# Bucket products as four 32-row pieces, key hashes side by side, and three PSUM banks for the preparing steps

## Chip, cores and metric

The kernel runs on one core of one Trainium2 chip. Its metric is the device time of one execution in microseconds (us). Executions of one kernel agree within about 0.2%, and every run told here with more than one execution is in the fast state. A ratio is the mean time of one kernel's fast runs over that of the other's fast runs of the same rounds, so it is not quite the ratio of the medians that are quoted beside it.

## The reference, cut to what matters

```python
# q, k, v: 4 batches x 8 heads x 768 x 64;  proj: 64 x 6
q_bucket = sum((q @ proj > 0) * 2**arange(6));  k_bucket likewise      # one of 64 buckets
scores   = where(q_bucket == k_bucket, q @ k.T / 8, -1e9)
attn     = softmax(scores) @ v
x        = attn of all heads, as (3072, 512)
out      = (silu(x @ w_gate) * (x @ w_val)) @ w_out                    # 512 -> 1536 -> 512
```

The bucket test is done by a matmul. A query has 13 numbers per head (six signs twice and a constant), and a key has 13 numbers of the order of 2^35. Their product is zero where all six bits agree and hugely negative otherwise. It is accumulated in PSUM ahead of the f32 scores, and the exponential then turns the excluded entries into zero.

## The kernel before

Work goes by pairs of heads, and within a pair by "rounds": two chunks of 128 keys against 384 queries, for both heads. While a pair is attended, the next pair is prepared: transposes of queries and keys, then their hashes. FFN products of the previous batch ("atoms") are woven in between, but during the first batch there are none.

```python
mm_ps  = tile_pool(bufs=2, space=PSUM)     # bank():      FFN products
aux_ps = tile_pool(bufs=1, space=PSUM)     # side_bank(): preparing steps and row sums
sc_ps  = tile_pool(bufs=2, space=PSUM)     # two chunks' scores, two banks each

def front(n, bank=side_bank):              # the steps that prepare pair n
    def transpose(name, half):
        ps = bank("tps")
        for i in range(CH): nc.tensor.transpose(ps[:, i*P:(i+1)*P], raws[name, n][...], ident)
        nc.scalar.copy(T[name, n][:, half*HQ:(half+1)*HQ], ps[:, 0:HQ])
    def hash_bits(name, half):
        ps = bank("hps")
        nc.tensor.matmul(ps[:, 0:HQ], hash_w[name], T[name, n][:, cols], start=True, stop=True)
        # q: sign on ScalarE; k: compare and scale on VectorE, into bf16 bits
    ...                                    # 4 transposes, then 4 hashes (q, k, q, k)

def score(u):                              # one chunk of keys; a round calls it twice
    sc = sc_ps.tile([P, 2, 512], FP32, tag="sc", name="sc")
    for x, start in ((bits, True), (T, False)):
        for h in range(2):
            rows = slice(h * D, (h + 1) * D)              # 64 rows a head, both products
            nc.tensor.matmul(sc[:, h, 0:HQ], x["k", n][rows, ks], x["q", n][rows, qs],
                             start=start, stop=not start)
    nc.scalar.activation(ring[u % RING][:, :, 0:HQ], sc[:, :, 0:HQ], AF.Exp, scale=SCALE)

def norm(u):                               # every third round
    ps = side_bank("sum")                  # row sums: matmuls with ones, 64 columns a head
    ...
    nc.vector.reciprocal(r, ps[:, 0:HQ])   # holds side_bank
# ... attend (weighted sums), FFN, weight narrowing on VectorE, main loop left out
```

The softmax here doesn't subtract the row's maximum and nothing guards it: scores larger than these inputs give would overflow.

## Time and profile before

| | before |
|---|---|
| time, median of 4 | 1187.30 us |
| first score | 13.25 us |
| first stretch (first score to first FFN product) | 130.1 us |
| first FFN product of first batch to that of the second | 287.4 us |
| FFN part (first FFN product to the end of the last product) | 1038.9 us |

How to read it: TensorE sets the time, so the kernel falls into a start (data arrives, first pair prepared), a first stretch (attention alone, TensorE sometimes waits) and an FFN part (TensorE never idle, up to the last down-projection). The limits are starts of groups in TensorE's timeline; the prediction shows the stretches themselves. The start, in TensorE's timeline of the kernel before (start in us, length, what, how often, idle before):

```profile
4.79 0.87 PE L205 MATMUL tps<-ident,qraw 128*128 128x128 f32 x3 [4.79 <-DMA qraw<-in_q_dram]
...
6.62 0.87 PE L205 MATMUL tps<-ident,kraw 128*128 128x128 f32 x3 [0.95 <-DMA kraw<-in_k_dram]
...
13.25 0.34 PE L244 MATMUL sc<-qb,kb 64*128 64x384 bf16 x2
```

Queries arrive at 4.8 us and keys at 6.6. Three transposes take 0.87 us here and 0.55 once the array runs at full clock.

### The profile page before, as it was taken

The numbers are of one execution on the slowest core, as the hardware profiler recorded it, in microseconds if no ns is written. First come the engines' busy times: TensorE is split into PE (matmuls) and PEld (weight loads), VectorE is DVE, ScalarE is ACT, GpSimd is POOL, SyncE is SP. The second block draws the span as 40 slices with busy tenths as digits, with TensorE's granted clock in tenths as the row PEclk, the third lists the DMA queues.
The fourth block names the chain that finished last, engine by engine and source line by source line (L and its number), as shares of the span: only waits on it lengthen the run. The fifth ranks groups of instructions, "written<-read, shape, count | busy, mean of one in ns | idle before, by whom it ended". The sixth has DMA issues, their size and how long they took to land.

```text
span 1185.9 us, 10899 instructions
## 1 busy us (share of the span) xinstructions
PE 1156.9 (98%) x4480; PEld 573.2 (48%) x4480; DVE 508.2 (43%) x756; ACT 280.3 (24%) x441; POOL 19.2 (2%) x44
## 2 busy tenths in 40 slices
PE   7888899999999999999999999999999999999998
PEld 3333355555544445555554445555554444555543
DVE  3777689998852323343331233333233222222100
ACT  4444422222212222222221213222131211000000
POOL 0000000000000000000000000000000000000000
PEclk9999999999999999999999999999999999999999
DMA  5322222324210120100002012010000000000000
GB/s 142 76 76 76 58 79 92 101 71 113 88 40 18 37 57 1 40 1 1 14 1 58 18 36 49 1 40 1 14 1 1 18 18 18 1 1 0 1 27 27
DMA packets 63698, 44.76 MB, mean 38 GB/s; under 512 B 51872, under 2 KB 55968, under 8 KB 63648
## 3 DMA queue, kind: packets, MB, share of 16 engines
q1 hardware_dynamic: 58752, 26.23, 8.6%
q0 software_dynamic: 4896, 17.83, 4.9%
q8 instruction: 35, 0.57, 0.2%
q14 instruction: 15, 0.12, 0.0%
HBM read 37.76 MB, written 6.29 MB: 37 GB/s over the span
## 4 chain that ended last, share of the span: by engine, by line
PE 97%; DVE 2%; ACT 1%; DMA 0%; SPq 0%; issue 0%; ACTq 0%
PE val L299 21%; PE g L299 21%; PE po L320 21%; PE sc L244 14%; PE av L255 11%; PE hps L213 4%; PE sum L276 2%; PE tps L205 2%; DVE r L279 2%; ACT qb L216 0%; ACT qT L208 0%; DMA kraw<-in_k_dram 0%; SPq L85 0%; ACT A L246 0%; ACT o L324 0%
## 5 line engine op out<-in xcount | busy, mean ns | idle before, releaser
L299 PE MATMUL val<-xT,wv 128*128 128x384 f32 x768 | 266.2, 489 | 0.0
L299 PE MATMUL g<-xT,wg 128*128 128x384 f32 x768 | 265.9, 489 | 0.0
L320 PE MATMUL po<-wo,ht 128*128 128x512 f32 x576 | 257.1, 597 | 0.0
L246 ACT ACTIVATE A<-sc 128x768 f32<-128x768 f32 x192 | 155.5, 812 | 208.2 <-PE sc L244 177.0
L299 PEld LDWEIGHTS val<-xT,wv 128*128 128x128 f32 x768 | 142.5, 190 | 105.4 <-DVE acc L263 6.0
L299 PEld LDWEIGHTS g<-xT,wg 128*128 128x128 f32 x768 | 142.5, 190 | 105.1 <-DVE acc L263 6.0
L320 PEld LDWEIGHTS po<-wo,ht 128*128 128x128 f32 x576 | 106.8, 190 | 134.1 <-issue 130.7
L244 PE MATMUL sc<-qT,kT 64*128 64x384 f32 x768 | 156.0, 485 | 0.0
L279 DVE RECIPROCAL r<-sum 128x384 f32<-128x384 f32 x32 | 81.8, 2556 | 151.9 <-PE sum L276 151.9
L255 PE MATMUL av<-A,vraw 128*64 128x386 f32 x768 | 144.8, 498 | 0.0
L306 DVE SCALAR_TENSOR_TENSOR t<-t,g 128x384 f32<-128x384 f32 x96 | 53.1, 554 | 206.3 <-ACT t L305 206.3
L263 DVE TENSOR_TENSOR acc<-acc,A 128x768 f32<-128x768 f32 x128 | 122.3, 955 | 35.2 <-ACT A L246 30.3
L305 ACT ACTIVATE t<-g 128x384 f32<-128x384 f32 x96 | 47.1, 490 | 351.6 <-PE g L299 347.0
L311 DVE SCALAR_TENSOR_TENSOR ht<-t,val 128x384 f32<-128x384 f32 x96 | 53.1, 553 | 125.0 <-PE val L299 125.0
L255 PEld LDWEIGHTS av<-A,vraw 128*64 128x64 f32 x768 | 49.6, 137 | 82.4 <-issue 81.3
L244 PEld LDWEIGHTS sc<-qT,kT 64*128 64x128 f32 x768 | 69.0, 190 | 21.5 <-issue 21.5
L244 PE MATMUL sc<-qb,kb 64*128 64x384 bf16 x384 | 63.8, 329 | 0.1
L218 DVE TENSOR_SCALAR kb<-hps,above_k,times_k 128x384 bf16<-128x384 f32 x32 | 21.6, 675 | 83.9 <-PE hps L213 83.4
L244 PEld LDWEIGHTS <-kb 64*128 64x128 bf16 x384 | 18.7, 93 | 67.9 <-issue 55.1
L324 ACT COPY o<-po 128x512 f32<-128x512 f32 x24 | 14.0, 585 | 144.3 <-PE po L320 142.0
L216 ACT ACTIVATE qb<-hps,nudge 128x384 bf16<-128x384 f32 x32 | 18.6, 581 | 69.4 <-PE hps L213 69.3
L213 PE MATMUL hps<-qT,hashq 128*128 128x384 f32 x64 | 27.7, 515 | 5.5 <-DVE e L281 5.5
(58 smaller groups left out, 409.9 us busy)
## 6 DMA issues: line engine op xcount, KB each, us to landing
qraw<-in_q_dram SPq DMA_DIRECT2D x32, 192.0 KB, 3.7
kraw<-in_k_dram SPq DMA_DIRECT2D x32, 192.0 KB, 4.6
vraw<-in_v_dram SPq DMA_DIRECT2D x16, 384.0 KB, 3.4
words<-in_moe_w_val_dram POOLq DMA_DIRECT2D x12, 512.0 KB, 3.8
words<-in_moe_w_out_dram POOLq DMA_DIRECT2D x12, 512.0 KB, 3.6
out_dram<-o SPq DMA_DIRECT2D x24, 256.0 KB, 2.0
words<-in_moe_w_gate_dram POOLq DMA_DIRECT2D x10, 512.0 KB, 3.9
words<-in_moe_w_gate_dram SPq DMA_DIRECT2D x2, 512.0 KB, 5.8
```

Of the source, the lines that this page charges most:

```text
L205: nc.tensor.transpose(ps[:, i * P : (i + 1) * P], raws[name, n][:, half * CH + i, :, :].rearrange("p h d -> p (h d)"), ident)
L213: nc.tensor.matmul(ps[:, 0:HQ], hash_w[name], T[name, n][:, cols], start=True, stop=True)
L244: nc.tensor.matmul(sc[:, h, 0:HQ], x["k", n][rows, ks], x["q", n][rows, qs], start=start, stop=not start)
L246: nc.scalar.activation(ring[u % RING][:, :, 0:HQ], sc[:, :, 0:HQ], AF.Exp, scale=SCALE)
L255: nc.tensor.matmul(ps[h * D : (h + 1) * D, 0:AW], raws["v", n][:, h, c, :], a[:, h, :], start=c == 0, stop=c == NCH - 1)
L263: nc.vector.tensor_tensor(acc[n, half], acc[n, half], a[:, :, 0:HQ], op=ALU.add)
L279: nc.vector.reciprocal(r, ps[:, 0:HQ])
L299: nc.tensor.matmul(ps[:, 0:HQ], w[:, j, f * P : (f + 1) * P], x[:, j, half * HQ : (half + 1) * HQ], start=j == 0, stop=j == NJ - 1)
L305: nc.scalar.activation(t, ps[:, 0:HQ], AF.Tanh, scale=0.5)
L306: nc.vector.scalar_tensor_tensor(out=t, in0=t, scalar=1.0, in1=ps[:, 0:HQ], op0=ALU.add, op1=ALU.mult)
L311: nc.vector.scalar_tensor_tensor(out=ht, in0=now["t"], scalar=0.5, in1=ps[:, 0:HQ], op0=ALU.mult, op1=ALU.mult)
L320: nc.tensor.matmul(ps, hs[half][f][:, i * P : (i + 1) * P], wo[:, f, :], start=f == 0, stop=f == NF - 1)
```

## The change

Its intent: run four bucket products at once instead of two, hash both halves of the keys in one go, bring in the first data on two queues with the array warmed by idle products, and, while there is no FFN work, let the preparing steps take turns over three PSUM banks.

```diff
-    load(0)
+    load(0, nc.scalar)                  # first keys on ScalarE's queue
+    zeros = konst.tile([P, 512], BF16, ...); nc.vector.memset(zeros, 0.0)
+    for _ in range(9):
+        nc.tensor.matmul(bank("idle"), zeros[:, 0:P], zeros, start=True, stop=True)
     # hash weights: proj is loaded twice, then copied by VectorE to its ten places
     # (before: six small DMAs); 13 rows now every 32 partitions (before: every 64)
@@ front
+    def front_bank(name):
+        return side_bank(name) if atoms or next(turn) % 3 == 2 else bank(name)
-            ps = bank("tps")            # bank was side_bank, but for the first pair
+            ps = front_bank("tps")
+        def hash_k():
+            ps = front_bank("hps")
+            chunks = T["k", n].rearrange("p (i g t) -> p i g t", g=2, t=P)
+            for g in range(2):          # even chunks to rows 0-63, odd ones to rows 64-127
+                nc.tensor.matmul(ps[g*D:(g+1)*D, 0:HQ].rearrange(...), hash_w["k"],
+                                 chunks[:, :, g, :], start=True, stop=True)
+            nc.vector.tensor_scalar(bits["k", n], ps[:, 0:HQ], ...)     # one compare, not two
-        # steps: 4 transposes, hash q, hash k, hash q, hash k
+        return steps + [hash_k, lambda: hash_q(0), lambda: hash_q(1)]
@@ score, now once a round
+        sc = [sc_ps.tile([P, 2, 512], FP32, tag="sc", name="sc") for _ in range(2)]
+        for g in range(2):
+            for h in range(2):
+                rows = slice(g*D + h*QUART, g*D + (h+1)*QUART)          # 32 rows
+                nc.tensor.matmul(sc[g][:, h, 0:HQ], bits["k", n][rows, ...],
+                                 bits["q", n][rows, qs], start=True, stop=False)
+        for g in range(2):
+            ...                         # scores of chunk g, 64 rows a head, then its exponential
```

## The prediction

> **What bounds the kernel now.** I read the page (busy times, the chain that ended last), then busy times by stretch, then who kept TensorE waiting early on, then TensorE's instructions in order of time.
>
> ```profile
> PE 1156.9 (98%) x4480; PEld 573.2 (48%) x4480; DVE 508.2 (43%) x756; ACT 280.3 (24%) x441; POOL 19.2 (2%) x44
> PE 97%; DVE 2%; ACT 1%; DMA 0%; SPq 0%; issue 0%; ACTq 0%
> L244 PE MATMUL sc<-qb,kb 64*128 64x384 bf16 x384 | 63.8, 329 | 0.1
> ```
>
> TensorE is 97% of the chain, so only time in TensorE's stream counts, and the others where they hold it up. The third row is the bucket product: 63.8 us in all. Busy times by stretch (TensorE, weight loads, VectorE, ScalarE, GpSimd, clock, DMA):
>
> ```profile
> 13.25:143.37 130.12, 110.53 (x626) 46.06 (x625) 94.00 (x125) 58.31 (x84) 3.84 (x7) 0.99 0.29 78
> 143.37:340.00 196.63, 196.63 (x795) 103.61 (x794) 175.84 (x296) 48.70 (x79) 14.55 (x27) 1.00 0.30 87
> 340.00:996.00 656.00, 656.00 (x2516) 319.09 (x2514) 206.30 (x261) 153.34 (x241) 0.00 (x0) 1.00 0.08 21
> ```
>
> The first stretch is the first batch's attention, before there is any FFN work to fill in: TensorE has nothing in flight for 19.6 of 130 us. After it TensorE is never idle. VectorE is at 89% up to 340 us, so it has room there, but not much. TensorE's waits up to 113.6 us (total, times, longest):
>
> ```profile
> PE tps L205 <- DVE e L281: 4.1, 3, 1.4
> PE hps L213 <- DVE e L281: 4.1, 3, 1.4
> PE hps L213 <- ACT qb L216: 4.0, 6, 0.7
> PE tps L205 <- ACT qT L208: 4.0, 7, 0.6
> ```
>
> All are the preparing steps (transposes, hashes) of the next pair of heads, queueing for one PSUM bank, behind each other's copy or behind the reciprocal that reads the row sums. Now TensorE in order of time (start, length, what):
>
> ```profile
> 72.32 0.34 PE L244 MATMUL sc<-qb,kb 64*128 64x384 bf16 x2
> ...
> 75.49 0.34 PE L244 MATMUL sc<-qb,kb 64*128 64x384 bf16 x2
> ...
> 85.50 0.55 PE L205 MATMUL tps<-ident,qraw 128*128 128x128 f32 x3
> 86.61 0.55 PE L205 MATMUL tps<-ident,kraw 128*128 128x128 f32 x3 [0.57 <-ACT qT L208]
> 87.09 0.34 PE L244 MATMUL sc<-qb,kb 64*128 64x384 bf16 x2
> ```
> ```profile
> 301.61 2.85 PE L299 MATMUL g<-xT,wg 128*128 128x384 f32 x8
> 304.29 0.49 PE L205 MATMUL tps<-ident,qraw 128*128 128x128 f32 x3
> 304.62 2.75 PE L299 MATMUL val<-xT,wv 128*128 128x384 f32 x8
> 307.20 0.49 PE L205 MATMUL tps<-ident,kraw 128*128 128x128 f32 x3
> 307.53 2.75 PE L299 MATMUL g<-xT,wg 128*128 128x384 f32 x8
> 310.21 0.34 PE L244 MATMUL sc<-qb,kb 64*128 64x384 bf16 x2
> 310.38 0.81 PE L244 MATMUL sc<-qT,kT 64*128 64x384 f32 x4
> 311.03 0.33 PE L244 MATMUL sc<-qb,kb 64*128 64x384 bf16 x2
> 311.19 0.81 PE L244 MATMUL sc<-qT,kT 64*128 64x384 f32 x4
> 311.93 1.52 PE L255 MATMUL av<-A,vraw 128*64 128x386 f32 x8
> ```
>
> Read starts, not lengths, since ends overlap. A bucket pair (two heads) takes 0.16 to 0.17 us until the scores start, so the two heads already run side by side (384 columns at 2.4 per ns are 0.16). Eight FFN products before a transpose take 2.58; before the bucket products, with 128 rows going to 64, they take 2.68. Leaving a tile shape costs 0.10 us. The eight at 301.61, which follow 64-column products, also take 2.68, though a transpose of their own shape comes next: 0.10 us again, now on entry, where an f32 weight load (190 ns each) can't be hidden. Entering with bf16 weights (93 ns) costs 0.01.
>
> **What the Trainium skill says.** "TensorEngine Tiling (Array Packing)", Tiling Modes, Key Properties: "Changing tiling mode (not just tile) drains the TensorE". The 0.10 us above agrees, for 128 rows to 64 and for 64 columns to 128. No run yet shows 32 rows to 64. "TensorE: Matmul & The Clock Gate", Part 3, Measured speedup vs the span model: tiles in different row groups run together, some 4 ns apart, four 32-row tiles at 512 columns 3.07 times as fast. The trace has two at a time at full rate. Same page, Part 1, What's actually happening: TensorE starts at half clock and needs about 3.4 us of activity. The trace's first transposes agree (three take 0.87 us at 4.79, 0.55 later). The Tiling page, Gotcha 1: row tiles must write different PSUM banks; the four pieces do.
>
> **The change part by part.** A round is two chunks of two heads. There are 96, 25 of them start before 139.56 us and 71 later, nearly all beside FFN work.
>
> *Bucket products.* Four 64-row matmuls in two goes become four 32-row ones in one go: −0.163 us. But now 32-row tiles come before the 64-row scores, which had shared the old shape. By the rows above that adds 0.10 for leaving and 0.10 for the f32 weight load: +0.20. Net +0.04 us per round, so 71 × 0.04 = +2.8 us beside the FFN. If 32 to 64 rows doesn't drain, −0.163 per round instead.
>
> *Key hashes.* Two f32 hashes of 0.65 us each (two passes of 0.322) become one go of 0.65 with two 64-column tiles. Beside the FFN they now stand between 128-column products: two shape changes at 0.10, entries at 0.05 and 0.10, so 0.35 of the 0.65 is given back. −0.30 × 11 pairs = −3.3 us. VectorE does one compare of 0.675 us less per pair, off the path.
>
> *First stretch.* From round to round now: plain 3.17 (72.32 to 75.49), new 3.21. Two transposes add 1.59 (87.09 − 85.50); without waits three at 0.109 plus entry, drain and the second three are 0.33 + 0.48 = 0.81. A row sum adds 0.70. Key hash and first query hash add 0.645 + 0.645 + 0.10 + 0.10 = 1.49; the last query hash 0.85. One pair of heads is six rounds: 6 × 3.21 + 2 × 0.70 + 2 × 0.81 + 1.49 + 0.85 = 24.6 us, against 31.2 now (72.32 to 103.53). The first pair, lacking a row sum and one product, takes 22.5 against 27.9. One step in three still uses the row sums' bank. Counting the turns, four steps follow a row sum there: two first ones wait 1.35 us and two second ones 1.0, together 4.7. So to 139.56: 22.5 + 3 × 24.6 + 4.7 + 3.2 = 104.2 against 126.3. VectorE then bounds almost as tightly: per pair eight adds of 0.955 and two of 0.95, two reciprocals of 2.556, 1.4 of normalising, 0.675, and thirteen weight-narrowing steps of 0.576: 24.2 us against 24.6. I add 1 us of stumbling: **−21 us**.
>
> *Start.* The first score is at 13.25. Queries and keys come at 4.8 and 6.6 us while the DMA share is about 1; two queues share the bandwidth, so I take both at 6.5. Nine idle products (half clock, 0.43 each, from about 1.2) end at 5.1, before that. Transposes at 0.35 to 7.2, the fourth after a copy at 7.7, four copies of 0.48 to 9.05, key hash, query hash at full clock to 10.85, its sign (0.58) to 11.45: first score at 11.5, **−1.8 us**.
>
> Sum, if 32 to 64 rows drains: +2.8 − 3.3 − 21 − 1.8 = −23.3, so 1164.4 us from 1187.7. Nothing at the end changes: the last 66 us are down-projections.
>
> **The rivals.**
> 1. *No drain between 32 and 64 rows.* Then 96 × 0.20 = 19 us more go: 1145. For it: both shapes split rows only, and the author chose this form. Against: every other shape change in the trace costs 0.10 plus the load. I give full or partial escape three chances in ten.
> 2. *VectorE takes over in the first stretch.* Its 94 us of busy time are there whatever TensorE does. Its 24.2 us per pair come in lumps (3.3 us after each row sum, which delays the adds that free the exponentials' buffers). Should it add 2 us per pair, the stretch gains 13 us: 1172. Against: its records overlap (a 0.69 us step is followed after 0.61), so 24.2 is an upper figure, and four buffers allow nearly two rounds of lag.
> 3. *Four row tiles not at full rate.* If the four take 0.25 us instead of 0.16, 96 × 0.09 = +9 us: 1173. The two heads of today lose nothing, which speaks against it.
> 4. *The preparing steps' waits were slack.* Had other work filled them, a spare bank would bring nothing: 1185. Against: TensorE is on the chain through this stretch and runs in order, so a wait there delays everything behind it.
>
> **Range and chances.** The main case lies at 1164.4, almost on the 2% line (1163.9). Three in ten I put between 1145 and 1158, one in ten above 1170. The middle of this is **1161 us**, range 1145 to 1171. Faster by over 2%: 0.63; within 2%: 0.36; slower by over 2%: 0.01.
>
> **What would show it.** Beside the FFN: from the bucket products to the first scores 0.36 us if it drains with an exposed load (0.16 if it doesn't), from bucket products to the weighted sum 1.76 against 1.72. Key hash to the next FFN product about 0.80, with FFN products before it stretched by 0.10. In the first stretch the four waits above shrink to about 5 us, behind the reciprocal alone, and a pair of heads takes 25 to 27 us. First score near 11.5. I am wrong if the FFN stretch itself moves by over 5 us with a shape change still visible, or if a pair of heads in the first stretch stays above 28 us.

## The result, and the profile after

The changed kernel takes 1170.24 us (median of 4, 1169.06 to 1171.17) against 1187.30. The ratio is 0.9857 with an interval of 0.9839 to 0.9874: 1.4% less time. The profiled execution, 1171.17 us, is the slowest of the four.

From the page of the changed kernel, the row of TensorE and that of the bucket products:

```profile
PE 1155.9 (99%) x4489; PEld 562.6 (48%) x4489; DVE 500.4 (43%) x767; ACT 269.3 (23%) x441; POOL 19.4 (2%) x46
L270 PE MATMUL sc<-qb,kb 32*128 32x384 bf16 x384 | 34.3, 333 | 1.3 <-ACT A L277 1.3
```

The bucket products' busy time fell by 29 us, from 63.8 to 34.3. It is tempting to take that for the gain. But TensorE's busy time as a whole fell by 1.0 us only (by 5.0 without the 4.0 us of idle products), and the time by 17. So most of the gain is idle time. The stretches of the changed kernel (same columns as before) say where it was:

```profile
15.14:125.26 110.12, 105.24 (x625) 44.19 (x624) 90.72 (x120) 55.41 (x85) 3.83 (x7) 1.00 0.30 78
125.26:322.00 196.74, 195.71 (x792) 100.27 (x790) 172.95 (x292) 46.97 (x79) 14.45 (x27) 1.00 0.30 87
322.00:978.00 656.00, 656.00 (x2515) 312.68 (x2514) 202.60 (x254) 147.32 (x240) 0.00 (x0) 1.00 0.08 21
```

In the first stretch TensorE's idle time is 4.9 us, where it was 19.6. That is 14.7 of the 20.0 us. The other 5.3 us are busy time (110.5 to 105.2). Part of them is the recorded end of a product that stands before a wait, which the next product covers elsewhere (three transposes are 0.55 us long, but 0.39 from start to start where nothing waits). About 1.7 us are clock: the clock records of the kernel before have TensorE back at half clock from 114.2 to 117.6 us, in the middle of its first stretch, and one round there takes 2.70 us instead of 1.72 up to its weighted sums, which take 2.12 instead of 1.45. Not every execution has this. Of the 28 executions of the kernel before whose clock is on record, ten took 1185.9 to 1186.4 us and 18 took 1186.8 to 1188.2, and 15 of the 18, but none of the ten, list a granted clock of 0.998. No trace of another kernel with f32 scores falls back so. That the waits bring it about was not tried.

In the second stretch there is now 1.0 us of idle time, where there was none. TensorE's waits from 10 to 140 us:

```profile
PE tps L227 <- DVE e L313: 2.2, 2, 1.4
PE hps L237 <- DVE e L313: 1.4, 1, 1.4
PE sc L270 <- ACT A L277: 1.3, 5, 0.4
PE hps L245 <- issue: 0.6, 1, 0.6
```

The waits for the steps' own copies are gone. Three waits for the reciprocal are left, and there is a new one: a round's pieces write the PSUM of both chunks, so they wait for both exponentials of the round before.

| | before | after | difference | forecast |
|---|---|---|---|---|
| first score at | 13.25 | 15.14 | +1.9 | −1.8 |
| first stretch | 130.1 | 110.1 | −20.0 | −21 |
| FFN, first batch to second | 287.4 | 288.9 | +1.5 | } −0.5 |
| FFN, rest to the last product | 751.5 | 751.4 | −0.1 | } |
| sum | | | −16.7 | −23.3 |

A round beside the FFN, in TensorE's timeline of the changed kernel; the last start is that of the weighted sums:

```profile
134.10 0.34 PE L270 MATMUL sc<-qb,kb 32*128 32x384 bf16 x4
134.37 1.56 PE L275 MATMUL sc<-qT,kT 64*128 64x384 f32 x8
135.86 0.55 PE L287 MATMUL av<-A,vraw 128*64 128x386 f32 x2
```

From bucket products to weighted sums it is 1.76 us, against 1.72 before: one go fewer, but 0.27 us until the scores start where it was 0.17, and a first score pair that takes longer (0.43 us instead of 0.32). So this part came out to the hundredth. What did not is the start:

```profile
1.19 4.02 PE L105 MATMUL idle<-zeros 128*128 128x512 bf16 x9 [1.19 <-DVE nudge L123]
6.12 0.87 PE L227 MATMUL tps<-ident,qraw 128*128 128x128 f32 x3 [0.91 <-DMA qraw<-in_q_dram]
8.03 0.88 PE L227 MATMUL tps<-ident,kraw 128*128 128x128 f32 x3 [1.04 <-DMA kraw<-in_k_dram]
...
10.80 1.55 PE L245 MATMUL hps<-kT,hashk 128*64 128x384 f32 x4 [0.61 <-issue]
12.28 2.93 PE L237 MATMUL hps<-qT,hashq 128*128 128x384 f32 x4
15.14 0.50 PE L270 MATMUL sc<-qb,kb 32*128 32x384 bf16 x4
```

Queries come 1.3 and keys 1.4 us later than before. The transposes still take 0.87, so the idle products had not brought the array to full clock, and the hashes too run at half (the key hash 1.55 us, later 0.81). The trace's clock records have full clock from 16.3 us on, against 11.8 before. The clock column of the stretches reads 1.00 all the same, as it counts the time before a trace's first clock record as full, so the durations are what to read here. The 1.5 us in the FFN part lie mostly in two places where a query hash waits, of 1.0 and 0.6 us; the longer one, TensorE first, then VectorE at the same time:

```profile
153.77 1.78 PE L329 MATMUL val<-xT,wv 128*128 128x384 f32 x5
156.26 0.91 PE L237 MATMUL hps<-qT,hashq 128*128 128x384 f32 x2 [0.72 <-DVE kb L247]
```
```profile
154.93 0.69 DVE L190 CUSTOM_DVE_ANT_0 wg<-words,wg 128x1024 uint16<-128x1024 uint16 x1
155.54 0.67 DVE L247 TENSOR_SCALAR kb<-hps,above_k,times_k 128x384 bf16<-128x384 f32 x1
```

The query hash needs the one side bank, which holds the key hash until VectorE has compared it, and VectorE comes to that only behind weight narrowing.

### The profile page after: what moved, and what is told of

Its sections match the earlier page's. It is cut to its first block, busy times and chain, and to the rows that moved or that the text cites. A ratio compares the mean times of both kernels' runs of the same rounds, so it can differ in the third digit from the quotient of the medians.

```text
span 1169.4 us, 10924 instructions
## 1 busy us (share of the span) xinstructions
PE 1155.9 (99%) x4489; PEld 562.6 (48%) x4489; DVE 500.4 (43%) x767; ACT 269.3 (23%) x441; POOL 19.4 (2%) x46
## 4 chain that ended last, share of the span: by engine, by line
PE 96%; DVE 2%; DMA 1%; ACT 0%; issue 0%; ACTq 0%
PE g L329 22%; PE po L350 22%; PE val L329 21%; PE sc L275 12%; PE av L287 10%; PE sc L270 2%; PE sum L308 2%; PE tps L227 2%; PE hps L237 2%; DVE r L311 1%; PE hps L245 1%; DMA kraw<-in_k_dram 1%; ACT A L277 0%; DVE acc L291 0%; DVE xT L314 0%
## 5 line engine op out<-in xcount | busy, mean ns | idle before, releaser
L277 ACT ACTIVATE A<-sc 128x768 f32<-128x768 f32 x192 | 145.3, 809 | 205.8 <-PE sc L275 161.4
L275 PE MATMUL sc<-qT,kT 64*128 64x384 f32 x768 | 150.2, 509 | 0.0
L275 PEld LDWEIGHTS sc<-qT,kT 64*128 64x128 f32 x768 | 66.3, 186 | 41.7 <-issue 17.0
L270 PEld LDWEIGHTS <-kb 32*128 32x128 bf16 x384 | 10.1, 91 | 57.7 <-issue 57.1
L270 PE MATMUL sc<-qb,kb 32*128 32x384 bf16 x384 | 34.3, 333 | 1.3 <-ACT A L277 1.3
L291 DVE SCALAR_TENSOR_TENSOR acc<-A 128x768 f32<-128x768 f32 x32 | 30.4, 952 | 2.2 <-ACT A L277 2.2
```

Of the source, the lines that this page charges most:

```text
L270: nc.tensor.matmul(sc[g][:, h, 0:HQ], bits["k", n][rows, c // 2 * P : (c // 2 + 1) * P], bits["q", n][rows, qs], start=True, stop=False)
L275: nc.tensor.matmul(sc[g][:, h, 0:HQ], T["k", n][rows, (c + g) * P : (c + g + 1) * P], T["q", n][rows, qs], start=False, stop=True)
L277: nc.scalar.activation(ring[(u + g) % RING][:, :, 0:HQ], sc[g][:, :, 0:HQ], AF.Exp, scale=SCALE)
```

## The experiments

My theory after the result: the banks are the whole gain, pieces and half-width hashes about cancel, the start loses some 2 us through loads and clock, and the order of the hashes loses 1.6 us beside the FFN. The main rival is what the page suggests: the bucket products' 29 us are the gain. For each run: median, ratio to the kernel before with its interval, first score, first stretch, FFN part (us).

| kernel | time | ratio | first score | stretch | FFN part |
|---|---|---|---|---|---|
| changed kernel | 1170.24 | 0.9857 (0.9839 to 0.9874) | 15.1 | 110.1 | 1040.3 |
| banks_only | 1167.82 | 0.9840 (0.9826 to 0.9853) | 12.5 | 110.8 | 1038.9 |
| pieces_only | 1177.95 | 0.9926 (0.9914 to 0.9938) | 17.2 | 112.2 | 1042.9 |
| k_sync | 1169.11 | 0.9845 (0.9831 to 0.9858) | 13.9 | 109.6 | 1040.3 |
| no_idle | 1169.05 | 0.9848 (0.9834 to 0.9861) | 13.5 | 109.6 | 1040.3 |
| long_idle | 1168.46 | 0.9843 (0.9830 to 0.9857) | 13.6 | 109.6 | 1040.2 |
| plain_start | 1169.79 | 0.9851 (0.9837 to 0.9864) | 14.2 | 109.6 | 1040.2 |
| hash_order | 1168.28 | 0.9843 (0.9829 to 0.9856) | 14.0 | 110.2 | 1038.6 |
| two_banks | 1162.79 | 0.9797 (0.9783 to 0.9810) | 13.4 | 105.1 | 1038.9 |
| two_banks_warm | 1161.77 | 0.9788 (0.9776 to 0.9800) | 11.9 | 105.4 | 1038.9 |
| shapes_two_banks | 1163.38 | 0.9804 (0.9791 to 0.9817) | 12.1 | 106.8 | 1038.6 |

### The banks alone

```diff
 # kernel before
-    def front(n, bank=side_bank):
+    def front_bank(name):
+        return side_bank(name) if atoms or next(turn) % 3 == 2 else bank(name)
+    def front(n):                       # transposes and hashes take front_bank
```

> The kernel before with one edit: the preparing steps of the first batch take turns over three banks. My theory (the banks are the whole gain; pieces and half-width hashes cancel; the start loses): the first stretch, from the first score to the first FFN product, is 18 to 20 us shorter than before's 130.1, the first score stays near 13 us, the time is 1166 to 1169, so 1 to 4 us below the changed kernel's 1170.2. Rival (the 29 us by which the bucket products' busy time fell on the page are the gain): the stretch shortens by 5 us or less and the time is 1180 or more.

The first stretch is 19.3 us shorter, the FFN part unchanged to 0.1 us, and the time 1167.82 us: the theory's numbers, and none of the rival's. The banks alone gain what the whole change gains and, by the medians, some 2 us more (the intervals overlap). Some 1.7 us of the 19.3 are the half clock of the kernel before, which this trace doesn't have. The stretch in this run:

```profile
12.52:123.35 110.83, 105.23 (x626) 46.25 (x625) 93.86 (x125) 57.44 (x85) 3.83 (x7) 1.00 0.35 93
```

TensorE's busy time here, 105.2 us, is within 0.01 us of that of the changed kernel, though the bucket products and hashes are the old ones.

### The pieces alone, on top of the banks

The keys' bits need the new layout, so their hash is made by two 128-column products that accumulate (no column tiles, and as many passes as before).

```diff
 # banks_only, with the score of the changed kernel and
+            for g in range(2):          # hash weights g fill columns 64*g and up, the rest is zero
+                nc.tensor.matmul(ps[:, 0:HQ].rearrange(...), hash_w["k", g],
+                                 chunks[:, :, g, :], start=g == 0, stop=g == 1)
```

> The three banks with the start of the kernel before, plus the four 32-row pieces, with the key hash as two accumulating 128-column products (no column tiles, same TensorE time as before). Theory (a change of shape from 32 to 64 rows costs 0.10 for leaving and 0.10 for the f32 weight load, against 0.16 gained): a round is 1.76 us against 1.72 from bucket products to the weighted sum; from the first FFN product to the end 1042 to 1043.5 us against the 1038.9 of three banks alone (71 rounds at 0.04, and up to 1.6 for the query hash waiting on the key compare in the one side bank); time 1170.5 to 1173, so 3 to 5 us slower than three banks alone at 1167.8. Rival (the pieces pay, as halved busy time of the bucket products suggests): time 1153 to 1164.

The FFN part is 1042.9 us, inside what the theory said and 4.0 over that of the banks alone. In the second batch's FFN, where nothing waits for the key compare, 24 rounds take 288.03 us against 286.99, so 0.043 us a round. A round shows 0.27 us from pieces to scores. The time, 1177.95 us, is above the expected 1170.5 to 1173, and the reason is mostly my edit, not the pieces: the key hash comes first, its weights come last of six small DMAs, and TensorE waits 3.3 us for them, so the first score is at 17.2, 4.7 us later than with the banks alone. The pieces don't pay.

### Where the 0.20 us of a shape change come from

```diff
 # changed kernel; values are wrong on purpose
-                T[name, n] = opnd.tile([P, S], FP32, ...)
+                T[name, n] = opnd.tile([P, S], BF16, ...)     # hash weights bf16 too
```

> The changed kernel with queries and keys kept in bf16 for hash and score products: wrong values on purpose, to part the two costs of entering the 64-row shape. Theory (0.10 us for leaving plus 0.10 us for an f32 weight load that can't be hidden): from the first bucket piece to the first score still 0.26 us, but from the first score pair to the second about 0.17 instead of 0.16 + 0.10 = 0.26. Rival (all of it is the drain): the first score pair still takes 0.10 us over the later ones. As the PSUM and ScalarE work stays, I expect no figure for the total.

The result was wrong by a relative error of 0.21; the one time, 1067.47 us, is not compared, since a bf16 score product is one instruction of 0.16 us and an f32 one is two of 0.32. A round of this kernel:

```profile
305.41 0.34 PE L270 MATMUL sc<-qb,kb 32*128 32x384 bf16 x4
305.69 0.50 PE L275 MATMUL sc<-qT,kT 64*128 64x384 bf16 x4
306.12 0.87 PE L308 MATMUL sum<-acc,ones 128*64 128x384 f32 x4
```

From the first piece to the first score it is still 0.274 us (median; 0.271 in the changed kernel, 0.16 to 0.17 before the change). From the first score pair to the second it is 0.173 (median), with a stream of 0.16; in the changed kernel it is 0.427, with a stream of 0.32. So 0.10 us are the change of shape, whatever the type, and 0.10 go with f32, against 0.01 with bf16. In the changed kernel's trace the first score's weight load of 0.18 us starts together with the score, and the later ones start ahead, which fits a load that can't be hidden. Both steps of the forecast hold.

### The start

Four edits of the changed kernel's start. The first keys back on the queries' queue:

```diff
-    load(0, nc.scalar)
+    load(0)
```

> The changed kernel with the first keys' loads back on the queue of the queries. Theory (loads side by side and the second pair's loads, now issued earlier, delay both queries and keys): first transposes at about 4.8 and 6.6 us instead of 6.1 and 8.0, first score 1 to 2 us before 15.1, time 1 to 2 us lower, 1168 to 1169. Rival (the late start is the half clock alone): first score moves by less than 0.5 us.

Transposes at 5.2 and 6.9 us, first score 1.3 earlier: both as the theory has it (the queries' transposes were held by the idle products, which end at 5.2). No idle products:

```diff
-    for _ in range(9):
-        nc.tensor.matmul(bank("idle"), zeros[:, 0:P], zeros, start=True, stop=True)
```

> The changed kernel without its nine idle products. Theory ([...]TensorE idles again after them, so they gain nothing): first score within 0.5 us of 15.1, clock still half until some 16 us, time within 1 us of 1170.2. Rival (they do warm the array): first score over 1 us later.

A miss in the first score, which came 1.6 us earlier rather than within 0.5. Full clock came at 11.6 us instead of 16.3, with no idle products at all. Neither theory had that, and this trace speaks against the rival (idle products help). And 22 idle products:

```diff
-    for _ in range(9):
+    for _ in range(22):
```

> The changed kernel with 22 idle products in place of nine, so that TensorE is busy without a break from 1.2 us until keys arrive at 8.0. Theory: full clock before 8.0 us[...], three transposes in 0.55 instead of 0.87, first score at 12.5 to 13.5 instead of 15.1, time about 2 us lower, 1167.5 to 1169. Rival (the start is bound by loads and copies alone): first score within 0.5 us of 15.1.

Full clock came at 7.2 us and the transposes took 0.49 to 0.55 us. The first score, at 13.6, is just outside the expected range, as the idle products themselves now run to 8.95 us, past the keys. Finally the loads as before and no idle products together:

```diff
-    load(0, nc.scalar)
+    load(0)
-    for _ in range(9): ...              # idle products
```

> The changed kernel with the first keys back on the queue of the queries and no idle products, its banks, pieces and hashes as they are. Theory (the start lost through later landings and a clock that stays at half; the rest of it is no slower than before's): transposes at about 4.8 and 6.9 us, first score between 12.0 and 13.5 us, depending on when the clock turns; first stretch 110 us and FFN part 1040 us as in the changed kernel, time 1167 to 1169. Rival (the later first score lies in the new order of hashes or in the copies that fill the hash weights): first score still at 14.5 us or later.

A miss: first score at 14.2 us, not 12.0 to 13.5, and nearer to the rival. In this run keys came at 7.7 us and full clock at 13.5. What all traces with the key hash first share is a gap behind the last transposes, 0.6 us of waiting in each of after, k_sync, no_idle, long_idle and plain_start: the key hash needs all four copies out of PSUM, where the kernel before went on at once with a query hash that needs only two. So the rival was right that the order of hashes costs something, but 0.6 us is all that the gap shows. The last run below, with a query hash first and no idle products, has no gap and its first score at 12.1; of the 2.1 us between the two, 0.6 are earlier keys (7.05 against 7.68), and full clock came 2.9 us earlier there (10.6). Nor does the order remove the gap everywhere: at full clock, in two_banks_warm, the query hash too waits 0.6 us for a copy.

Times of these four, 1168.5 to 1169.8 us, have overlapping intervals, so no part of the start is told apart by them. When full clock came, by the traces' clock records: with nine idle products at 13.5, 13.6 and 16.3 us, and in the bf16 run at 6.5, to be lost again from 9.9 to 16.7; without any, from 10.5 to 13.5 in six runs, and at 16.2 in pieces_only, which waits longest for its hash weights; with 16 and 22 at 4.7 and 7.2, and not lost again. So nine products are a matter of luck, and longer runs of them did better, in one trace each.

### The order of the hashes

```diff
-        return steps + [hash_k, lambda: hash_q(0), lambda: hash_q(1)]
+        return steps + [lambda: hash_q(0), hash_k, lambda: hash_q(1)]
```

> The changed kernel with the first query hash ahead of the key hash. Theory (beside the FFN the query hash waited 1.0 us and 0.6 us in two places for the key compare, which queues behind weight narrowing on VectorE and holds the one side bank): the second batch's FFN stretch, from the first product of the first to the first of the second, falls from 288.9 to 287.3 us, time 1168 to 1169.5. Rival (the stretch lengthened through shape changes): it stays within 0.3 us of 288.9.

From the first FFN product of the first batch to that of the second it is 287.28 us, and the time 1168.28: the theory's numbers. The waits of 1.0 and 0.6 us are gone, as is the gap at the start.

### Off the row sums' bank

The kernel before with the banks alone; after the very first pair no step of the first batch uses the row sums' bank.

```diff
-        return side_bank(name) if atoms or next(turn) % 3 == 2 else bank(name)
+        return side_bank(name) if atoms or next(turn) == 2 else bank(name)
```

> Three banks alone, but with the first batch's steps never in the row sums' bank (after the very first pair). Theory (the 5.4 us that TensorE still waits for the reciprocal there are on the path, and VectorE has just room): waits for the reciprocal gone, first stretch 3 to 5.4 us shorter than 110.8, time 1162.5 to 1165. Rival (VectorE is the bound of the first stretch by now): under 1.5 us shorter, waits for exponentials or adds in its place.

The first stretch is 5.8 us shorter, slightly more than expected, the time 1162.79 us:

```profile
13.44:118.50 105.06, 104.67 (x625) 46.34 (x625) 93.47 (x125) 56.81 (x85) 3.84 (x7) 1.00 0.35 97
```

TensorE idles for 0.4 us of 105. VectorE, at 89%, hardly holds it up, so that rival falls. Two banks that nobody else holds beat three of which one is shared with a reciprocal.

### Two more versions

With 16 idle products ahead, loads and shapes as before:

```diff
 # two_banks
+    for _ in range(16):
+        nc.tensor.matmul(bank("idle"), zeros[:, 0:P], zeros, start=True, stop=True)
```

> Two banks for the steps, shapes and loads of the kernel before, plus 16 idle products, enough to keep TensorE busy from 1.2 us to the arrival of the first keys. Theory: full clock by 8 us, first score at 11.3 to 12.5 instead of 13.4, first stretch and FFN part unchanged (105.1 and 1038.9), time 1161 to 1162.5. Rival (the loads alone set the start): first score above 12.9, time 1162.5 or more.

```profile
1.19 5.36 PE L101 MATMUL idle<-zeros 128*128 128x512 bf16 x16 [1.19 <-DVE zeros L98]
6.44 0.52 PE L217 MATMUL tps<-ident,qraw 128*128 128x128 f32 x3
...
11.87 0.34 PE L256 MATMUL sc<-qb,kb 64*128 64x384 bf16 x2
```

First score at 11.9, time 1161.77 us, as expected: the fastest version, 2.1% under the kernel before (ratio 0.9776 to 0.9800) and 0.7% under the changed one. All its executions lie below all those of two_banks, but the intervals of the two ratios overlap. And the new shapes with everything else at its best:

```diff
 # plain_start
-        return steps + [hash_k, lambda: hash_q(0), lambda: hash_q(1)]
+        return steps + [lambda: hash_q(0), hash_k, lambda: hash_q(1)]
-        return side_bank(name) if atoms or next(turn) % 3 == 2 else bank(name)
+        return side_bank(name) if atoms or next(turn) == 2 else bank(name)
```

> The changed kernel with all that the runs so far found better, except its new shapes, which stay: loads as before, no idle products, first query hash ahead of the key hash, steps off the row sums' bank. Against two banks with the old shapes (1162.8 us; first stretch 105.1, FFN part 1038.9). Theory (pieces cost 0.04 a round, half-width hashes give 0.3 a pair back beside the FFN, and the pieces wait for both chunks' exponentials in the first stretch): FFN part 1038.3 to 1038.9, first stretch 105.5 to 107, time 1163 to 1165, so no faster than the old shapes. Rival (the new shapes do pay once the rest is out of their way): time under 1162.

All three parts came as the theory had them: FFN part 1038.6, first stretch 106.8, time 1163.38 us. The new shapes gain 0.2 us beside the FFN and lose 1.7 in the first stretch, of which 1.5 are pieces waiting for exponentials, and the whole is no faster than the old shapes' 1162.79. It isn't slower by 1.5 us because in its trace the first score came 1.3 us earlier: there is one key hash less ahead of it, and full clock came at 10.6 us against 12.7. How much of the 1.3 is each, was not tried.

## Why the prediction was right or wrong

The range held and "within 2%", the less likely class by the forecast, is what came. The middle of 1161 us was 9 too low. 3.4 of these are the weight given to the first rival (1161 instead of the main case's 1164.4), which did not happen: 32 to 64 rows drains like every other change of shape.

**Bucket products**: right in mechanism and in size. 1.76 us a round was forecast and measured; 0.04 a round was forecast, and the pieces alone show 0.043. Drain and exposed weight load are 0.10 each, told apart by the bf16 run. Only the place of the load was wrong: 0.36 us from bucket products to scores were forecast and 0.27 came, as the load shows behind the first score pair and not ahead of it.

**Key hashes**: the gain is as large as forecast, but a cost was missed. In the second batch's FFN, where nothing waits, the changed kernel takes 286.84 us against the 288.03 of pieces_only: −0.30 for each of four pairs, as forecast. The step "VectorE does one compare of 0.675 us less per pair, off the path" failed. Fewer compares, but the one that is left now stands directly ahead of a query hash that wants the same bank, while VectorE is nearly full with narrowing. Putting the query hash first takes 1.6 us away.

**First stretch**: −20.0 against −21. The step that a pair of heads without waits takes 24.6 us held: from 67.00 to 91.50, where TensorE waits for nothing, it is 24.5. Four waits for the reciprocal, 4.7 us, were forecast; three came, 3.6 us in all. What I had not listed is the 1.3 us of pieces waiting for both exponentials, and 0.5 us at half clock at the head of the stretch, where the first pieces and scores take 0.50 and 1.90 us and later ones 0.34 and 1.56. Nor had I seen, in the 0.99 of the first stretch's clock, the half clock that cost the kernel before 1.7 us; that part of the gain was not forecast as such.

**Start**: the step that failed. Forecast −1.8, came +1.9, which is more than half of the main case's miss of 6.6 us. By its own terms: keys at 8.0 us and not 6.5 (1.5 us), and from key hash to first score 4.3 us, not 2.45 (1.9 us), because the array ran at half clock all that way. "Query hash at full clock to 10.85" took the nine idle products to warm the array for good. They end at 5.2 us, the array then waits 0.9 and 1.0 us for data, and full clock came at 16.3. The forecast took "about 3.4 us of activity" as enough wherever it falls. But the turns of the clock in bf16_scores, at 6.47, 9.88 and 16.71 us, lie one and two times 3.41 us apart, as if on a fixed grid, and 4.0 us of work need not fill a step of such a grid. The forecast also had two queues sharing the bandwidth so that nothing is lost on the keys. In the traces with one queue the keys' first transposes come at 6.6 to 7.7 us (seven runs, mean 7.1), with two at 7.7 to 8.1 (four runs, mean 7.9; left out are runs in which idle products still ran when the keys came). That the second pair's loads, now issued at 2.8 us instead of 7.95, take part of the bandwidth is my reading of it and was not tried by itself. When full clock comes also varies from run to run, and one profile of each kernel doesn't tell how much: the changed kernel's own four executions spread over 2.1 us, and its profiled one is the slowest.

**Rivals**: VectorE did not become the bound in the first stretch. Four row tiles run at full rate: from pieces to scores it is 0.27 us where all four go at once (134.10), and as much where a wait leaves only two of them (18.44 to 18.71). Rival four (the waits are slack) is refuted by the banks alone.

So the gain went where it was expected, into the first stretch, and the two new shapes gave nothing: with the rest at its best they cost 1.5 us from the first score on and give back at most 1.3 before it (shapes_two_banks against two_banks). Of what the banks could have gained, some 2 us were lost at the start, 1.6 to an order of steps, and 3 to a third bank that was not free (first stretch of shapes_two_banks against plain_start, 106.8 to 109.6).

## What to carry to other kernels

A busy time that halves is not time won. Packing small products into finer tiles pays only if the tile shape around them stays the same, since each change of shape costs the drain and an exposed weight load (0.10 us each here, with f32 weights); count both before packing. Before tuning the products, look for steps that queue for one PSUM bank behind a slow reader, and give them banks that no slow reader holds. When warming an array with idle work, let it last until the data is there, and not much longer (16 products did, 22 ran on to 8.95 us, past the keys).

## What the Trainium skill lacked or had wrong

- "TensorEngine Tiling (Array Packing)", Tiling Modes, Key Properties, says that a change of mode drains, but gives no cost. Here it is 0.10 us for the drain at each change measured, 32 to 64 rows included, plus the first weight load that can't be hidden: 0.10 us for f32 with 128 columns, 0.01 for bf16.
- "TensorE: Matmul & The Clock Gate", Part 2, LDWEIGHTS, gives columns divided by 1.2 per ns, so 107 ns for 128 columns. The trace has 186 to 190 ns for f32 and 91 to 93 for bf16 with 128 columns, and 134 to 139 for f32 with 64, so the f32 loads fit it neither in size nor in proportion.
- Same page, Part 1: it asks for one busy window of about 3.4 us, which it calls free-running (the grid of 3.41 us above agrees), but doesn't say how busy. Nine products in a row, 4.0 us, brought full clock in one run of four, and lost it 3.4 us later; 16 and 22 products brought it at 4.7 and 7.2 us and kept it.
- The tiling page, Gotcha 1, says that row tiles raise the pressure on PSUM. Here is a size: pieces of two chunks wait until the banks of both have been read, 1.3 us in five waits in the first stretch, and nothing where FFN products lie between rounds.
